# A chunked gated recurrence in front of two expert layers: inclusive gate sums, column pairs on TensorE, rows and logits in one product, and elementwise work on GpSimd

## The chip, the core and the metric

The kernel runs on one core of a Trainium2 chip. A core has five engines that run side by side and wait for one another through semaphores: TensorE (PE in the profile; PEld is its weight load), VectorE (DVE), ScalarE (ACT), GpSimd (POOL) and SyncE (SP), which here issues most of the transfers. The metric is the device time of one execution in microseconds.

## The reference

Three stages follow one another. Only the first is changed.

```python
def _attn_ref(q, k, v, f_logit):            # (4, 8, 768, 48) each
    f = 1.0 / (1.0 + np.exp(-f_logit))
    for t in range(S):
        state = f[:, :, t, :, None] * state + np.einsum('bhd,bhe->bhde', k[:, :, t], v[:, :, t])
        y[:, :, t] = np.einsum('bhd,bhde->bhe', q[:, :, t], state)

def _moe_ref(x, ...):                       # x: (3072, 384), 8 experts, 2 per token
    noisy_logits = x @ w_gate + np.log1p(np.exp(x @ w_noise)) * noise
    # the two best experts per token, softmax over the two
    # out += weight * (relu(x @ w1[e]) @ w2[e])

def _moe2_ref(x, ...):                      # rms norm, then a gated feed-forward layer, width 1536
    return (silu(xn @ w_gate) * (xn @ w_val)) @ w_out
```

## The kernel before

The recurrence is cut into 24 chunks of 128 positions: 4 batches of 6 chunks, all 8 heads at a time. The heads lie in pairs (HP = 4 pairs): one head of a pair on partitions 0 to 63 (48 of them used), the other on 64 to 127. A chunk n passes through these steps, each a function in the code:

- `decay`: the gates' logarithms and their running sum along the chunk. A clip (L325, VectorE), an exponential and a logarithm (L327, L329, ScalarE), a scan (L331, VectorE). Tile `cs`.
- `prep`: keys times exp(sum), queries times exp(-sum): `KT` (L358) and `QT` (L363), both on VectorE.
- `keys`: the keys turned by TensorE, copied to `Ks`.
- `scores`: the products of keys and queries, 8 heads (L384), in two halves; VectorE multiplies each of two banks by the causal mask, `AM` (L389).
- `state`: keys times values, for a pair of heads in one product (L398); `carry` adds the old state on VectorE (`su`, L413) and scales it on GpSimd (`Ss`, L415). In the first chunk of a batch VectorE does it alone, in the last there is none.
- `inter`: queries times old state (L424), and `attend`: masked scores times values (L432), into the same bank; four heads of one side are taken first, then four of the other. ScalarE copies the bank to `yT`.
- `rows`: the result turned and written to memory (`xd`); `logit` and `logit_turn`: the routing logits as four narrow products (L453), a copy, a turn, and a sum on VectorE (L462).

After every four chunks a `router` picks the experts for 512 tokens, in parts that `safe()` takes off a list, twice in a chunk. When the first 8 chunks are routed, their tokens are fetched back by indirect transfers that GpSimd issues (L719) and turned (`turn`), and the expert layers can begin. `expert_stream` issues these: units of an upper product (N = 256 tokens, L645) and a lower one (384 columns, also L645), each product in three parts of split precision. Weights come in half-loads, split into a high and a low part by ScalarE (L207) and by VectorE or GpSimd (L209).

TensorE runs in program order. The loop at the end of the main function sets that order: at each `yield` of `gla_stream` it adds the yield's cost to a debt, and from the moment that the first tokens are turned and the list of router steps is empty, it pays the debt at half the rate (RATIO = 0.5) with pieces of `expert_stream`. So expert products stand between the recurrence's. After the last chunk expert work runs alone. The orders of VectorE, ScalarE and GpSimd come from a scheduler, and stand fixed in the program too.

## Time and profile before

| | |
|---|---|
| median of 3 runs | 1114.31 us (1112.85 to 1114.65) |
| the profiled execution, own time | 1113.67 us |
| its span, first to last instruction | 1111.9 us |
| PE, DVE, ACT, POOL busy | 1071.9, 695.3, 490.6, 355.8 us |
| matmul records | 6861 |

The profile is one execution. Its page gives busy shares; a busy PE is not PE at its peak, since matmuls overlap. Windows give the busy time of each engine in a stretch; the timeline lists instructions in order of time; lines group instructions of one code line and one shape.

### The profile page before, as it was taken

To read this page: it belongs to the slowest core of one execution; us is meant where nothing else is said; L and a number is where in the kernel's file an instruction comes from. 1 tells how busy PE (TensorE), PEld (TensorE's weight loads), DVE (VectorE), ACT (ScalarE), POOL (GpSimd) and SP (SyncE) were. 2 spreads that over 40 slices of the span, in tenths; PEclk is the share of its full clock that TensorE was granted. 3 is DMA by queue.
4 is the path that set the end of the run, shared out by engine and by line. 5 is a ranking of instruction groups with operands and counts; after the bars stand their busy time and mean duration, and the time that the engine had idled before them with its cause. 6 is when DMAs were issued, how large, how long until landed. Compare 5 with 4: busy or idle time off the path is not lost.

```text
span 1111.9 us, 18697 instructions
## 1 busy us (share of the span) xinstructions
PE 1071.9 (96%) x6861; PEld 969.2 (87%) x6861; DVE 695.3 (63%) x1637; ACT 490.6 (44%) x1148; POOL 355.8 (32%) x415
## 2 busy tenths in 40 slices
PE   8999997999999999999999999999999999999997
PEld 5787777999989999999999988788888888888886
DVE  7999986977777554565666769745345344354332
ACT  5766543566655443444454555423223223232211
POOL 5544622434354434444546433120030020110000
PEclk9999998999999999999999999999999999999999
DMA  9986612677776443444443434120020110110001
GB/s 293 259 256 204 203 45 61 220 250 242 244 231 207 155 126 89 143 140 129 153 150 120 152 122 135 43 71 15 1 86 1 41 45 1 57 29 1 29 1 32
DMA packets 104873, 133.00 MB, mean 120 GB/s; under 512 B 8576, under 2 KB 80788, under 8 KB 104772
## 3 DMA queue, kind: packets, MB, share of 16 engines
q1 hardware_dynamic: 95203, 112.28, 31.5%
q0 software_dynamic: 9568, 19.43, 6.4%
q8 instruction: 56, 0.92, 0.3%
q14 instruction: 46, 0.37, 0.1%
HBM read 107.66 MB, written 24.02 MB: 118 GB/s over the span
## 4 chain that ended last, share of the span: by engine, by line
PE 67%; DVE 10%; DMA 10%; ACT 5%; issue 4%; POOL 3%; SPq 0%; another core or an unknown queue 0%; DVEq 0%; ACTq 0%; POOLq 0%
PE bank L645 63%; DMA raw<-in_moe_w_dram 5%; DMA xg<-xd,stoka 2%; DVE wlo L209 2%; PE bank L171 2%; PE bank L432 1%; DMA xg<-xd,stokr 1%; ACT whi L207 1%; POOL xg L719 1%; DVE AM L389 1%; DVE cs L331 1%; DVE xlo L633 1%; POOL Ss L415 1%; ACT L L327 1%; POOL hs L337 1%
## 5 line engine op out<-in xcount | busy, mean ns | idle before, releaser
L645 PE MATMUL bank<-xhi,whi 128*128 128x256 f32 (+8 forms) x1008 | 335.7, 333 | 2.2 <-ACT xhi L632 1.6
L645 PE MATMUL bank<-xlo,whi 128*128 128x256 f32 (+8 forms) x1008 | 334.9, 332 | 0.6 <-DVE xlo L633 0.5
L645 PE MATMUL bank<-xhi,wlo 128*128 128x256 f32 (+8 forms) x1008 | 334.7, 332 | 0.0
L645 PE MATMUL bank<-whi,hhi 128*128 128x384 f32 (+2 forms) x728 | 246.8, 339 | 8.1 <-ACT y L764 6.1
L645 PE MATMUL bank<-whi,hlo 128*128 128x384 f32 (+2 forms) x728 | 245.5, 337 | 0.0
L645 PE MATMUL bank<-wlo,hhi 128*128 128x384 f32 (+2 forms) x728 | 245.1, 337 | 0.0
L645 PEld LDWEIGHTS bank<-xhi,whi 128*128 128x128 f32 x1008 | 190.1, 189 | 22.4 <-ACT xhi L632 2.5
L645 PEld LDWEIGHTS bank<-xhi,wlo 128*128 128x128 f32 x1008 | 190.3, 189 | 17.3
L645 PEld LDWEIGHTS bank<-xlo,whi 128*128 128x128 f32 x1008 | 190.0, 189 | 16.9 <-DVE xlo L633 1.2
L719 POOL DMA_INDIRECT xg<-xd,stokr x139 | 133.9, 963 | 153.3 <-ACT hhi L747 125.2
L748 DVE SCALAR_TENSOR_TENSOR hlo<-bank,hhi 128x256 fp32r<-128x256 f32 (+7 forms) x192 | 83.2, 434 | 113.0 <-ACT hhi L747 92.2
L645 PEld LDWEIGHTS bank<-whi,hhi 128*128 128x128 f32 (+2 forms) x728 | 133.4, 183 | 13.8 <-ACT y L764 7.7
L209 DVE TENSOR_TENSOR wlo<-raw,whi 128x384 fp32r<-128x384 f32 (+1 forms) x312 | 135.6, 472 | 12.0 <-ACT whi L207 7.4
L747 ACT ACTIVATE hhi<-bank 128x256 fp32r<-128x256 f32 (+7 forms) x192 | 74.8, 389 | 147.3 <-PE bank L645 127.7
L645 PEld LDWEIGHTS bank<-wlo,hhi 128*128 128x128 f32 (+2 forms) x728 | 133.4, 183 | 6.2
L207 ACT ACTIVATE whi<-raw 128x256 fp32r<-128x256 f32 (+1 forms) x320 | 127.0, 452 | 24.7 <-DMA raw<-in_moe_w_dram 22.1
L645 PEld LDWEIGHTS bank<-whi,hlo 128*128 128x128 f32 (+2 forms) x728 | 132.8, 182 | 3.3
L838 DVE TENSOR_TENSOR sg<-bank,sg 128x512 f32<-128x512 f32 x72 | 49.7, 690 | 117.3 <-ACT sg L837 117.3
L789 POOL DMA_INDIRECT xg<-yd,slots x40 | 44.3, 1107 | 241.2 <-ACT hhi L841 207.6
L837 ACT ACTIVATE sg<-bank 128x512 f32<-128x512 f32 x72 | 43.0, 597 | 143.1 <-PE bank L645 134.4
L841 ACT ACTIVATE hhi<-sg 128x512 fp32r<-128x512 f32 x72 | 45.4, 630 | 116.2 <-DVE sg L839 116.0
L719 POOL DMA_INDIRECT xg<-xd,stoka x64 | 65.8, 1029 | 80.8 <-ACT hhi L747 68.4
(170 smaller groups left out, 1184.5 us busy)
## 6 DMA issues: line engine op xcount, KB each, us to landing
raw<-in_moe_w_dram SPq DMA_DIRECT2D x64, 768.0 KB
kq<-in_kq_dram SPq DMA_DIRECT2D x23, 512.0 KB
yd<-y SPq DMA_DIRECT2D x48, 192.0 KB
ft<-in_f_logit_dram SPq DMA_DIRECT2D x23, 256.0 KB
Vs<-in_v_dram SPq DMA_DIRECT2D x24, 192.0 KB
xd<-x SPq DMA_DIRECT2D x24, 192.0 KB
raw<-in_moe_w_gate_dram SPq DMA_DIRECT2D x6, 768.0 KB
raw<-in_moe_w_val_dram SPq DMA_DIRECT2D x6, 768.0 KB
```

The source lines that it names most:

```text
L171: nc.tensor.transpose(p, x, i)
L207: nc.scalar.activation(hi[:, j], raw[:, j], AF.Copy)
L209: e.tensor_tensor(lo[:, j], raw[:, j], hi[:, j].bitcast(F32), op=OP.subtract)
L327: nc.scalar.activation(l, f, AF.Exp, scale=-1.0)
L645: nc.tensor.matmul(o, a, b, start=start and i == 0, stop=stop and i == 2)
L719: paced(nc.gpsimd.indirect_dma_start(out=b.xg[i][:, k_], out_offset=None, in_=table, in_offset=bass.IndirectOffsetOnAxis(ap=rows_of[:, k_, ...
L747: mark[0] = nc.scalar.activation(hhi[:, :N], p[:, :N], AF.Relu).ins
L748: mark[1] = nc.vector.scalar_tensor_tensor(hlo[:, :N], p[:, :N], 0.0, hhi[:, :N].bitcast(F32), op0=OP.max, op1=OP.subtract).ins
L789: paced(nc.gpsimd.indirect_dma_start(out=y, out_offset=None, in_=ya if n < GROUP else yd, in_offset=bass.IndirectOffsetOnAxis(ap=at_, axis ...
L837: nc.scalar.activation(sg, ps[0], AF.Sigmoid)
L838: nc.vector.tensor_tensor(sg, ps[0], sg, op=OP.mult)
L841: mark[0] = nc.scalar.activation(hhi, sg, AF.Copy).ins
```

## The change

The running sum now takes in the gate of the chunk's first position, so that the chunk's own total is the last column of exp(-sum): GpSimd copies it to `hs` and `carry` multiplies by it, and the four small instructions that made the weight `w` go. The sum's cap becomes a cap of 4.7e18 on exp(sum), within the key product. The clip of the gates goes from VectorE to GpSimd, as do the query product of every odd chunk and one product of five of the six routings. The scores of 8 heads go to one tile of two banks and are masked by one instruction. `state` and `attend` take the two heads of a pair one after the other, each on its own half of TensorE's columns; `carry` works on the two halves of the partitions apart. `rows` and the logits come from one product of `yT` with a matrix of 96 picking and 16 weight columns (`columns`). The order in a chunk is scores, rows, inter, keys, state, attend, and routing, fetches, weight loads and turns are put one to four chunks earlier. The key product becomes a scalar-tensor-tensor instruction.

```diff
-GATE_MAX, GATES_MAX = 39.0, 60.0
+GATES_MAX = 42.0
+KEYS_MAX = 4.7e18
...
-    ROUTE = (0, 2, 4)
+    ROUTE = (0, 1, 2)
...
-    BANK = {"T": "04", "t": "0", "A0": "1", "A1": "2", "Y": "3", "U": "5", "X": "7", "R": "6"}
-    SHARED = {"T": "0", "A0": "1", "A1": "2", "Y": "3", "U": "7", "X": "7", "R": "0",
-              "h": "4", "t": "0", "acc": "56"}
+    BANK = {"T": "0", "K": "4", "t": "0", "Y": "3", "U": "5", "X": "7", "R": "6"}
+    SHARED = {"T": "0", "K": "7", "Y": "3", "U": "0", "R": "7", "h": "4", "t": "0", "acc": "56"}
...
-        nc.vector.tensor_scalar(f, f, -GATE_MAX - 1.0, None, op0=OP.max)
+        nc.gpsimd.tensor_scalar(f, f, -GATES_MAX - 1.5, None, op0=OP.max)
         yield
         nc.scalar.activation(l, f, AF.Exp, scale=-1.0)
         yield
         nc.scalar.activation(l, l, AF.Ln, bias=1.0)
         yield
         nc.vector.tensor_tensor_scan(cs.rearrange("p a t -> p (a t)"),
-                                     l.rearrange("p a t -> p (a t)"),
-                                     chain[:, s].rearrange("p a t -> p (a t)"), 0.0,
-                                     op0=OP.add, op1=OP.min)
-        yield
-        if s.stop == HP:
-            nc.gpsimd.tensor_copy(hs[:, 0, n], st["L", n][:, :, 0])
-            nc.gpsimd.tensor_copy(hs[:, 1, n], st["cs", n][:, :, P - 1])
-            if n % NCH:
-                e = wk.tile([P, HP], F32, name="e", bufs=3)
-                nc.gpsimd.tensor_tensor(e, hs[:, 1, n - 1], hs[:, 0, n], op=OP.add)
-                nc.scalar.activation(e, e, AF.Exp, scale=-1.0)
-                w = wk.tile([P, HP, 2], F32, name="w", bufs=4)
-                nc.gpsimd.tensor_tensor(w, e[:, :, None].to_broadcast([P, HP, 2]),
-                                        upper[:, None, :].to_broadcast([P, HP, 2]), op=OP.mult)
-                st["w", n - 1] = w
+                                     chain[:, s].rearrange("p a t -> p (a t)"),
+                                     l.rearrange("p a t -> p (a t)"), 0.0,
+                                     op0=OP.mult, op1=OP.add)
...
-        st["K"] = nc.vector.tensor_tensor(st["KT", n][:, s], Ek, st["kq", n][:, s, 0],
-                                          op=OP.mult).ins
+        st["K"] = nc.vector.scalar_tensor_tensor(st["KT", n][:, s], Ek, KEYS_MAX,
+                                                 st["kq", n][:, s, 0], op0=OP.min,
+                                                 op1=OP.mult).ins
         yield
         st["e"] = nc.scalar.activation(cs, cs, AF.Exp, scale=-1.0).ins
         yield
-        nc.vector.tensor_tensor(st["QT", n][:, s], cs, st["kq", n][:, s, 1], op=OP.mult)
+        (nc.gpsimd if n % 2 else nc.vector).tensor_tensor(
+            st["QT", n][:, s], cs, st["kq", n][:, s, 1], op=OP.mult)
+        if s.stop == HP:
+            nc.gpsimd.tensor_copy(hs[:, n], st["cs", n][:, :, P - 1])
...
-    def scores(n, part):
+    def scores(n):
         QT = st["QT", n]
         KT = st["KT", n]
-        if part == 0:
-            st["pA", n] = [cut(bank(f"A{g}"), HP, P) for g in range(2)]
-        ps = st["pA", n]
-        for h in range(4 * part, 4 * part + 4):
+        p = pa.tile([P, 2, HP, P], F32, name="scores")
+        for h in range(H):
             o = 64 * (h % 2)
-            nc.tensor.matmul(ps[h % 2][:, h // 2, :], KT[o:o + D, h // 2, :],
+            nc.tensor.matmul(p[:, h % 2, h // 2, :], KT[o:o + D, h // 2, :],
                              QT[o:o + D, h // 2, :], start=True, stop=True)
-        if part:
-            for g in range(2):
-                t = wk.tile([P, HP, P], F32, name=f"AM{g}")
-                nc.vector.tensor_tensor(t, ps[g], mask[:, None, :].to_broadcast([P, HP, P]),
-                                        op=OP.mult)
-                st["AM", n, g] = t
+        t = st["AM", n] = wk.tile([P, H, P], F32, name="AM")
+        nc.vector.tensor_tensor(t, p.rearrange("p g a t -> p (g a) t"),
+                                mask[:, None, :].to_broadcast([P, H, P]), op=OP.mult)
...
-        pU = cut(bank("U"), HP, 2 * D)
+        pU = cut(bank("U"), HP, D)
         for a in range(HP):
-            nc.tensor.matmul(pU[:, a], Ks[n % NK][:, 2 * a:2 * a + 2, :],
-                             Vs[n % NV][:, 2 * a * D:2 * (a + 1) * D], start=True, stop=True)
+            for g in range(2):
+                h = 2 * a + g
+                nc.tensor.matmul(pU[64 * g:64 * (g + 1), a], Ks[n % NK][:, h],
+                                 Vs[n % NV][:, h * D:(h + 1) * D], start=True, stop=True,
+                                 skip_group_check=True)
...
-        w = st["w", n]
-        sn = Ss[(c + 1) % 2].rearrange("p a b d -> p (a b) d")[:, :, :D]
-        u = st["pU", n].rearrange("p a (b d) -> p (a b) d", b=2)
-        wb = w.rearrange("p a b -> p (a b)")[:, :, None].to_broadcast([P, H, D])
-        if c:
-            t = wk.tile([P, H, D], F32, name="su", bufs=1)
-            nc.vector.tensor_tensor(t, u, Ss[c % 2].rearrange("p a b d -> p (a b) d")[:, :, :D],
-                                    op=OP.add)
-            st["C"] = nc.gpsimd.tensor_tensor(sn, t, wb, op=OP.mult).ins
-        else:
-            nc.vector.tensor_tensor(sn, u, wb, op=OP.mult)
+        u = st["pU", n]
+        t = None if c == 0 else wk.tile([P, HP, D], F32, name="su", bufs=1)
+        for g in range(2):
+            o = slice(64 * g, 64 * (g + 1))
+            wb = hs[o, n, :, None].to_broadcast([64, HP, D])
+            sn = Ss[(c + 1) % 2][o, :, g, :D]
+            if c:
+                nc.vector.tensor_tensor(t[o], u[o], Ss[c % 2][o, :, g, :D], op=OP.add)
+                st["C"] = nc.gpsimd.tensor_tensor(sn, t[o], wb, op=OP.mult).ins
+            else:
+                nc.vector.tensor_tensor(sn, u[o], wb, op=OP.mult)
...
-    def attend(n, g):
+    def attend(n):
         c = n % NCH
         pY = st["pY", n]
-        for h in range(g, H, 2):
-            nc.tensor.matmul(pY[64 * g:64 * (g + 1), h // 2, :], Vs[n % NV][:, h * D:h * D + 64],
-                             st["AM", n, g][:, h // 2, :], start=not c and h == g,
-                             stop=h == H - 2 + g, skip_group_check=True)
-        if g:
-            y = wk.tile([P, HP, P], F32, name="yT")
-            nc.scalar.activation(y, pY, AF.Copy)
-            st["yT", n] = y
+        for a in range(HP):
+            for g in range(2):
+                h = 2 * a + g
+                nc.tensor.matmul(pY[64 * g:64 * (g + 1), a, :], Vs[n % NV][:, h * D:h * D + 64],
+                                 st["AM", n][:, g * HP + a, :], start=not c and a == 0,
+                                 stop=a == HP - 1, skip_group_check=True)
+        y = wk.tile([P, HP, P], F32, name="yT")
+        nc.scalar.activation(y, pY, AF.Copy)
+        st["yT", n] = y
...
-        p = cut(bank("T"), HP, P)
+        p = cut(bank("T"), HP, NX + 2 * E)
         for a in range(HP):
-            flip(p[:, a, :], y[:, a, :], ident)
-        x = wk.tile([P, H, D], F32, name="x")
-        nc.scalar.activation(x, p.rearrange("p a (b d) -> p (a b) d", b=2)[:, :, :D], AF.Copy)
-        nc.sync.dma_start(xd[n * P:(n + 1) * P, :], x)
-
-    def logit(n):
-        y = st["yT", n]
-        p = cut(bank("X"), P)
-        for a in range(HP):
-            nc.tensor.matmul(p[32 * a:32 * (a + 1), :], wgn[:, a, :], y[:, a, :],
-                             start=True, stop=True, skip_group_check=True)
-        t = wk.tile([P, P], F32, name="lgT")
-        nc.scalar.activation(t, p, AF.Copy)
-        st["lgT", n] = t
-
-    def logit_turn(n):
-        p = cut(bank("X"), P)
-        flip(p, st["lgT", n], ident)
-        nc.vector.tensor_reduce(lg[:, n], p.rearrange("p (a e) -> p e a", a=HP)[:, :2 * E],
-                                axis=AX.X, op=OP.add)
+            nc.tensor.matmul(p[:, a, :], y[:, a, :], columns[:, a, :], start=True, stop=True)
+        x = wk.tile([P, HP, NX], F32, name="x")
+        nc.scalar.activation(x, p[:, :, :NX], AF.Copy)
+        nc.sync.dma_start(xd[n * P:(n + 1) * P, :], x.rearrange("p a x -> p (a x)"))
+        nc.vector.tensor_reduce(lg[:, n], p.rearrange("p a e -> p e a")[:, NX:], axis=AX.X,
+                                op=OP.add)
...
+        (nc.gpsimd if n1 < NT else V).tensor_tensor(
+            rh, rh, names[:, 2 * n0:2 * n1, None].to_broadcast([P, 2 * ng, nst]), op=OP.mult)
...
-                scores(i, 0)
-                safe()
-                yield 0.87
-                scores(i, 1)
-                yield 0.87
+                scores(i)
+            safe()
+            yield 1.1
             if i == 0:
                 run(prep, 1)
                 for n in range(2, GATES):
                     after_prep(decay, n)
-            if valid(i):
-                state(i)
-                yield 0.86
-            safe()
             if valid(i - 1):
                 rows(i - 1)
-                yield 0.43
+                yield 1.0
             if valid(i):
                 inter(i)
-                carry(i)
-                yield 0.87
-            if valid(i - 1):
-                logit(i - 1)
-            if valid(i):
-                attend(i, 0)
-                yield 0.8
+                yield 1.0
+            safe()
             if valid(i + AHEAD):
                 run(prep, i + AHEAD)
             if valid(i + 1):
                 keys(i + 1)
-                yield 0.43
+                yield 0.5
             if valid(i):
-                attend(i, 1)
-                yield 0.57
-            if valid(i - 1):
-                logit_turn(i - 1)
+                state(i)
+                carry(i)
+                attend(i)
+                yield 1.6
...
-            if i in (6, 8):
+            if i in (4, 6):
                 start_loads()
-            if 8 <= i < 16:
+            if 6 <= i < 14:
                 take_part(0)
...
 
     for m in range(NT // GROUP - 1):
-        i = m * GROUP + GROUP + 2
+        i = m * GROUP + GROUP + 1
         for o in ROUTE + ((ROUTE[-1] + 1,) if (m + 1) * GROUP == NTA else ()):
             at(i + o, lambda m=m: route(m))
-    for j, fns in enumerate(blocks[0].fetches):
-        for k_, fn in enumerate(fns):
-            at(16 + j, fn)
-    for fn in blocks[0].turns:
-        at(19, fn)
+    for i, fn in enumerate(blocks[0].fetches + [blocks[0].turns]):
+        at(13 + i, lambda fns=fn: [fn() for fn in fns])
```

TensorE, one chunk early in the program, before and after. Banks are matmul results; `ident` marks a turn.

```order
L398 MATMUL bank_370<-Vs_125,Ks_122 128x96 x4
L171 MATMUL bank_375<-ident,yT 128x128 x4
L424 MATMUL bank_383<-QT,Ss_130 128x128 x4
L453 MATMUL bank_391<-yT,wgn 32x128 x4
L432 MATMUL bank_383<-AM_366,Vs_125 64x128 x4
L171 MATMUL bank_409<-ident,KT 128x128 x4
L432 MATMUL bank_383<-AM_368,Vs_125 64x128 x4
L171 MATMUL bank_421<-ident,lgT 128x128
```

```order
L380 MATMUL scores<-QT,KT 128x128 x8
L442 MATMUL bank_342<-columns,yT 128x112 x4
L421 MATMUL bank_351<-QT,Ss_132 128x128 x4
L173 MATMUL bank_364<-ident,KT 128x128 x4
L394 MATMUL bank_370<-Vs_127,Ks_124 64x48 x8
L431 MATMUL bank_351<-AM,Vs_127 64x128 x8
```

Before, the eight score products (four rows to a bank, not shown) precede these; the state product stood ahead of `inter` and the two halves of `attend` apart. Now state and attend stand together at the end, with narrow products, two for each pair.

GpSimd, where the first expert units stand beside the recurrence (late chunks), before and after. L719 and L702 are the indirect loads of expert tokens, Ss the new state.

```order
L415 TENSOR_TENSOR Ss_129<-su,w 128x8x48
L719 DMA xg<-xd,stoka 128x96
L338 COPY hs<-cs 128x4
L415 TENSOR_TENSOR Ss_130<-su,w 128x8x48
L415 TENSOR_TENSOR Ss_129<-su,w 128x8x48
L415 TENSOR_TENSOR Ss_130<-su,w 128x8x48
L719 DMA xg<-xd,stoka 128x96 x56
```

```order
L412 TENSOR_TENSOR Ss_131<-su,hs 64x4x48 x2
L702 DMA xg<-xd,stoka 128x96 x4
L211 TENSOR_TENSOR wlo_1857<-raw,whi_1856 128x256
L702 DMA xg<-xd,stoka 128x96
L358 TENSOR_TENSOR QT<-cs,kq 128x512
L361 COPY hs<-cs 128x4
L412 TENSOR_TENSOR Ss_132<-su,hs 64x4x48 x2
```

The loads for expert units stood behind the last state; now they stand between states, with weight splits and query products.

## Rows read from the trace of the kernel before

**Rows 1.** windows, all engines; stretch, us, busy us (records), clock, DMA share, GB/s

```profile
7.20:120.40 113.20, 105.32 (x1011) 86.55 (x1010) 105.55 (x251) 75.36 (x178) 55.82 (x104) 0.98 0.87 256
120.40:174.10 53.70, 50.18 (x520) 42.20 (x519) 43.93 (x127) 25.40 (x62) 23.29 (x35) 1.00 0.31 93
174.10:183.10 9.00, 3.17 (x38) 2.56 (x37) 4.74 (x18) 2.91 (x9) 3.03 (x4) 0.84 0.15 44
```

**Rows 2.** windows, the score products of L384 alone

```profile
7.20:120.40 113.20, 20.22 (x257) 16.20 (x257) 0.98 0.87 256
```

**Rows 3.** timeline, PE, one chunk; start us, us, instruction

```profile
154.81 1.16 PE L384 MATMUL bank<-QT,KT 48*128 48x128 f32 x16
155.91 1.13 PE L398 MATMUL bank<-Vs,Ks 128*128 128x96 f32 x8
156.87 0.60 PE L171 MATMUL bank<-ident,yT 128*128 128x128 f32 x4
157.31 1.06 PE L424 MATMUL bank<-QT,Ss 128*128 128x128 f32 x8
158.30 0.43 PE L453 MATMUL bank<-yT,wgn 128*32 128x128 f32 x8
158.65 1.09 PE L432 MATMUL bank<-AM,Vs 128*64 128x128 f32 x8
159.67 0.66 PE L171 MATMUL bank<-ident,KT 128*128 128x128 f32 x4
160.26 1.09 PE L432 MATMUL bank<-AM,Vs 128*64 128x128 f32 x8
161.28 0.33 PE L171 MATMUL bank<-ident,lgT 128*128 128x128 f32 x1
161.53 0.71 PE L384 MATMUL bank<-QT,KT 48*128 48x128 f32 x8
```

**Rows 4.** timeline, PE, late chunks

```profile
165.54 1.58 PE L432 MATMUL bank<-AM,Vs 128*64 128x128 f32 x16
170.47 0.28 PE L645 MATMUL bank<-xhi,whi 128*128 128x256 f32 x1
170.59 0.28 PE L645 MATMUL bank<-xlo,whi 128*128 128x256 f32 x1
```

**Rows 5.** lines, DVE, 7.2 to 174.1; shapes, count, busy us, mean ns, idle before

```profile
L389 DVE TENSOR_TENSOR AM<-bank,mask 128x512 f32<-128x512 f32 x48 | 31.1, 677 | 2.2 <-PE bank L384 2.2
L363 DVE TENSOR_TENSOR QT<-cs,kq 128x512 f32<-128x512 f32 x23 | 17.0, 741 | 1.1 <-ACT cs L361 1.1
L325 DVE TENSOR_SCALAR ft<-ft 128x512 f32<-128x512 f32 x23 | 12.0, 529 | 0.0
L413 DVE TENSOR_TENSOR su<-bank,Ss 128x384 f32<-128x384 f32 x16 | 8.7, 546 | 0.0
L541 DVE TENSOR_TENSOR r_rh<-r_rh,names 128x448 f16<-128x448 f16 x4 | 3.0, 748 | 0.0
```

**Rows 6.** lines, POOL, 7.2 to 174.1

```profile
L415 POOL TENSOR_TENSOR Ss<-su,w 128x384 f32<-128x384 f32 x16 | 21.7, 1357 | 30.0 <-DVE su L413 13.4 <-DVE r_oh L521 5.6 <-DVE r_mx L482 4.7
L209 POOL TENSOR_TENSOR wlo<-raw,whi 128x384 fp32r<-128x384 f32 x4 | 4.5, 1131 | 1.5 <-ACT whi L207 1.4
L118 POOL CAST irowh<-irow 128x128 f16<-128x128 f32 x1 | 0.3, 333 | 0.0
```

**Rows 7.** timeline, DVE and POOL, three places

```profile
111.57 1.21 POOL L415 TENSOR_TENSOR Ss<-su,w 128x384 f32<-128x384 f32 x1 [1.71 <-DVE su L413]
112.01 1.05 DVE L325 TENSOR_SCALAR ft<-ft 128x512 f32<-128x512 f32 x1
...
118.17 0.41 DVE L325 TENSOR_SCALAR ft<-ft 128x512 f32<-128x512 f32 x1
...
158.32 0.83 POOL L415 TENSOR_TENSOR Ss<-su,w 128x384 f32<-128x384 f32 x1 [4.72 <-DVE r_mx L482]
```

**Rows 8.** timeline, POOL, an indirect load

```profile
173.36 0.94 POOL L719 DMA_INDIRECT xg<-xd,stoka  x1 [0.30 <-issue]
```

More of the change, by code (lines that the diff above doesn't have):

```diff
@@ L1 @@
+import math
 from contextlib import ExitStack
@@ L90, in tile_gated_attention_moe_ffn @@
     ones = cp.tile([P, P], BF16, name="ones")
-    upper = cp.tile([P, 2], F32, name="upper")
     names = ep.tile([P, 2 * NT], F16, name="names")
@@ L105, in constants @@
         yield
-        nc.vector.memset(upper, 0.0)
-        nc.vector.memset(upper[0:64, 0:1], 1.0)
-        nc.vector.memset(upper[64:128, 1:2], 1.0)
+        nc.gpsimd.tensor_copy(
+            pick_x.rearrange("p a (b d) -> p a b d", b=2),
+            ident.rearrange("p (b d) -> p b d", b=2)[:, None, :, :D].to_broadcast([P, HP, 2, D]))
         yield
@@ L155, in bank @@
             i = turns[use] = turns.get(use, -1) + 1
-        return pp.tile([P, 512], F32, name="bank" + b[i % len(b)])
+        k_ = b[i % len(b)]
+        return (late["pp"] if k_ in "12" else pp).tile([P, 512], F32, name="bank" + k_)
     def cut(t, *dims):
@@ L271, in tile_gated_attention_moe_ffn @@
     chain = gp.tile([P, HP, P], F32, name="chain")
-    wgn = gp.tile([P, HP, 32], F32, name="wgn")
+    NX = 2 * D
+    columns = gp.tile([P, HP, NX + 2 * E], F32, name="columns")
+    pick_x = columns[:, :, :NX]
+    pa = gla.enter_context(tc.tile_pool(name="pa", bufs=1, space=PSUM))
     NK, NV = AHEAD + 1, LOADS + 2
@@ L369, in keys @@
             return
-        p = cut(bank("T"), HP, P)
+        p = cut(bank("K"), HP, P)
         for a in range(HP):
@@ L440, in rows @@
     def rows(n):
         y = st["yT", n]
-        p = cut(bank("T"), HP, P)
+        p = cut(bank("T"), HP, NX + 2 * E)
         for a in range(HP):
-            flip(p[:, a, :], y[:, a, :], ident)
-        x = wk.tile([P, H, D], F32, name="x")
-        nc.scalar.activation(x, p.rearrange("p a (b d) -> p (a b) d", b=2)[:, :, :D], AF.Copy)
-        nc.sync.dma_start(xd[n * P:(n + 1) * P, :], x)
-    def logit(n):
-        y = st["yT", n]
-        p = cut(bank("X"), P)
-        for a in range(HP):
-            nc.tensor.matmul(p[32 * a:32 * (a + 1), :], wgn[:, a, :], y[:, a, :],
-                             start=True, stop=True, skip_group_check=True)
-        t = wk.tile([P, P], F32, name="lgT")
-        nc.scalar.activation(t, p, AF.Copy)
-        st["lgT", n] = t
@@ L616, in check @@
         bad = rp.tile([P, 4], F32, name="bad")
-        for c, most in enumerate((GATE_MAX, GATES_MAX)):
-            V.tensor_reduce(bad[:, c:c + 1], hs[:, c].rearrange("p n a -> p (n a)"), axis=AX.X,
-                            op=OP.max)
-            V.tensor_scalar(bad[:, c:c + 1], bad[:, c:c + 1], most, None, op0=OP.is_gt)
+        V.tensor_reduce(bad[:, 1:2], hs.rearrange("p n a -> p (n a)"), axis=AX.X, op=OP.min)
+        for c in range(2):
+            V.tensor_scalar(bad[:, c:c + 1], bad[:, 1:2], math.exp(-GATES_MAX), None, op0=OP.is_lt)
         V.tensor_reduce(bad[:, 2:3], early, axis=AX.X, op=OP.max)
@@ L1023, in gla_stream @@
             load_f(3)
-            nc.sync.dma_start(wgn, moe_w_both)
+            nc.sync.dma_start(columns[:, :, NX:], moe_w_both[:, :, :2 * E])
             for t in Vs:
@@ L1136, in tile_gated_attention_moe_ffn @@
     banks[0] = FULL
+    late["pp"] = main.enter_context(tc.tile_pool(name="pp2", bufs=1, space=PSUM))
     wp2 = main.enter_context(tc.tile_pool(name="wp2", bufs=1))
```

10 lines of the change are left out of this document (4 added, 6 removed).

## The prediction

> **What bounds the kernel now.** I read the page first. PE is busy 96% of the span, but that is a mean over two stages: a recurrence of 24 chunks up to 174 us, in which hardly any expert work runs, and expert layers afterwards, which the change doesn't touch. So time can be gained in two ways: a shorter recurrence, or expert work done inside it. I then took windows over the recurrence. Chunks 0 to 15 take 113.2 us [rows 1]: the score products have 16 records a chunk and 257 stand in that window [rows 2], so it is 16 chunks of 7.07 us. In it PE is busy 105.32 us and DVE 105.55 us [rows 1]: 6.58 and 6.60 us a chunk, both 93%. Neither has room, so a chunk gets shorter only if both get less to do. Chunks 16 to 23 take 53.7 us, 6.71 us each, and there DVE is down to 82%, since the gates and keys of later chunks are done, while PE stays at 93% [rows 1]. From 174.1 to 183.1 the last results and routing steps follow one another with PE busy 3.17 of 9.00 us [rows 1]. Expert work at its full rate starts at 183.1 us; until then two upper units are done, 18 products of 0.12 us from start to start [rows 4], 2.2 us.
>
> The timeline of one chunk without routing shows what PE does, by the starts [rows 3]: scores 1.10, state 0.96, rows 0.44, inter 0.99, logits 0.35, attend 1.02, keys 0.59, attend 1.02, turn of the logits 0.25; 6.72 us in all. I use starts and not durations, since each group's last matmul overlaps the next group.
>
> **PE, part by part.** Scores 1.10, inter 0.99 and keys 0.59 stay. The logits' 0.35 and the turn's 0.25 go. The turn of rows becomes a full product with 112 columns, shaped like inter with 128: 0.99 x 112/128 = 0.87 (bounds: 0.44, as the turn, and 0.99, as inter). Attend now alternates between the two halves of the columns. Where its halves happened to follow each other directly, 16 passes took 1.58 us, against 1.09 for 8 [rows 3, 4]; the second half cost only 0.49. The halves overlap, then, and finer alternation should let them do so throughout. I take 1.10, the time of the 16 alternating passes of the scores (bounds 1.02 and 1.58). State becomes 16 passes of half the width instead of 8: between 0.48, half of today's, and 1.92, twice; no row shows it. I take 0.65, near the lower end, as the alternating passes are the nearest row. Sum: 1.10 + 0.87 + 0.99 + 0.59 + 0.65 + 1.10 = 5.30 us, 1.4 us less than now.
>
> **DVE, part by part, per chunk.** The clip goes: 12.0 us in 23 instructions, 0.52 each [rows 5]. Half the query products go: 0.741/2 = 0.37. One routing product of 0.748 goes in five of the six routings, 0.16 per chunk. Two maskings of 0.677 become one of twice the size: between no gain and 0.2; I take 0.10. The addition of 0.546 is cut into two on half the partitions, each with half the columns: between no loss and 0.546; I take 0.10 over the chunks, since only 16 of 24 have it. The key product keeps its size and its place, and the scan also: nothing. Sum: 6.60 - 0.52 - 0.37 - 0.16 - 0.10 + 0.10 = 5.55 us.
>
> **What GpSimd gives back.** It gets the clip: 128x512 with one input. A conversion of 128x128 took 0.333, the nearest row with one input [rows 6]; by width it would be 1.33, without growth 0.33, and I take the middle, 0.8 (upper bound 1.5, a two-input product of this width). The query product: a two-input product of 128x384 took 1.131, so 1.51, every second chunk 0.75 [rows 6]. The routing product about 0.3 a chunk. Together 1.85 us more, while four tiny instructions go. GpSimd has room (55.82 of 113.2 us busy), but not beside every DVE instruction. A clip on DVE that started 0.44 us after a state product on GpSimd took 1.05 us and ended 0.28 us after that product did (113.06 and 112.78 us); another took 0.41 [rows 7]. The state product takes 0.83 left alone and 1.357 on average [rows 6, 7]. They exclude each other. Today this costs the clips 0.529 - 0.41 = 0.12 us on average for 0.55 us of state products per chunk: a fifth. A fifth of 1.85 is 0.35 (bounds: nothing, if all of it falls beside DVE's PSUM work, and 1.85). DVE: 5.9 us a chunk, more than PE's 5.3, so DVE sets the pace in chunks 0 to 15. At the present 93% that is 6.3 us.
>
> **The sum.** Chunks 0 to 15: 16 x 6.3 = 101 us, from 7.2 to 108 us. By the order of the changed program, 108 upper products (256 columns, 0.12 us) and 54 lower ones (384 columns, 0.18 by width) then stand between the recurrence's matmuls before its last attend: 13.0 + 9.7 = 22.7 us. Chunks 16 to 23: 8 x 5.30 = 42.4, less 2.5 for two chunks without state and keys, plus 22.7 = 62.6 us of PE work; at 93%, 67.4 us. The recurrence ends at 175.6 us. The tail with its PE idle time is gone, as the last routing steps of the loop are due in chunks 21 to 23 instead of 22 to 26, and expert work fills the rest. Against now: 183.1 - 175.6 = 7.5 us earlier, and 22.7 - 2.2 = 20.5 us of expert work ahead. 28 us in all. 1111.9 - 28 = 1083.9 us of span; the execution's own time lies 1.8 us above its span and 0.6 below the median, so 1086 us.
>
> Transfers: DMA is 87% busy in chunks 0 to 15 [rows 1] at 256 GB/s. A chunk needs 1.15 MB, 4.5 us at that rate, below 6.3; weights that start earlier add some. I cost it at nothing; if chunks fell to 5.5 us, DMA would be next.
>
> **Rivals.** *The lock (20%).* GpSimd's new work doesn't fit beside DVE's PSUM instructions; most of the 1.85 us comes back as waiting, on either engine. Rows 7 speak for it, and that GpSimd was idle half the time against it. DVE at 6.5 us and 93%: 7.0 us a chunk, 112 us; the late chunks at 9.0, 72 us, since weight splits on GpSimd come in there: end at 191 us, 8 later than 183.1, with 20.5 us ahead: 12.5 us gained, 1101 us. The Trainium skill, page "SBUF — State Buffer", section "Who interferes with whom", states that GpSimd shares a pair of SBUF ports with DVE as an exclusive lock, held for the whole instruction, against any DVE instruction with two SBUF inputs. By that rule moving the clip off DVE would free nothing where scan and key product follow each other closely; this trace agrees as to the blocking [rows 7], not as to how often it strikes. By the rule in full the time is this rival's, by the fifth of above the forecast's.
>
> *PE sets the pace (20%).* The lock costs nothing, and the early chunks run at 5.3/0.93 = 5.7: 91 us; the late ones at 96%, 65 us: end at 163.5, 40 us gained, 1074 us.
>
> *The column halves don't overlap (4%).* Attend stays at 2.04 and state takes 1.3: PE 6.9 us, 7.07 a chunk as now, the late chunks 78 us or more: end at 198 us, 5 us gained, 1109 us. The 1.58 us of rows 4 speaks against it.
>
> *Slower: the state's round trip (6%).* State product, addition on DVE, scaling on GpSimd and inter follow each other, and now only attend, scores and rows, some 3 us of PE, lie between state and the next inter; before, it was nearly a whole chunk. The scaling queues behind clips, query products and, in late chunks, up to five indirect loads of 0.94 + 0.30 us [rows 8]. In early chunks: 0.65 + 0.65 + 1.5 behind a query product + 2.7 for two scalings both blocked like today's 1.357 + 0.99 + 0.59 keys = 7.1 us; with 6.2 us of loads in front, over 10 in late ones. It decides if the round trip exceeds 6.3 us in most chunks, and makes the kernel slower when early chunks average 7.6 and late ones 10: end at 209 us, 26 later, 20.5 ahead: 1119 us. Against it: only 16 of 24 chunks have the trip, and expert products lengthen the slack in late chunks.
>
> **Numbers.** The forecast itself has 50%, 1078 to 1094 us. With the lock and PE as bound the range is 1070 to 1106 us; outside are the unpaired halves, the slow round trip and the ends of the two rivals. 0.2% (about what a measurement tells from no change) is 2 us. Faster 0.92, the same 0.03, slower 0.05.
>
> **What would show it.** Attend near 1.1 us in the timeline, state near 0.65, a rows product near 0.9: PE's part. Chunks 0 to 15 in 101 us with DVE above 90% busy: DVE's part; if DVE is below 85% there and PE waits for Ss, it is the round trip; if clips or scans are stretched beside GpSimd, the lock. Upper products between scores from chunk 15 on, PE above 90% there, and no idle stretch after the last attend. The forecast is wrong if the recurrence ends after 190 us, or if a later stage gives the lead back, by waiting for weights before 300 us.

## The result, and the profile after

The changed kernel takes 1130.9 us (median of 4 runs, 1127.8 to 1132.1) against 1114.5 before: a ratio of 1.014 (95% interval 1.012 to 1.016). The forecast was 1086 us, range 1070 to 1106. Its profiled execution has a span of 1129.5 us, 17.6 more than before.

The two stages of the recurrence, in the windows of the changed kernel (columns as in [rows 1]), end where the scores of chunk 16 begin and behind the last rows product:

```profile
8.20:149.30 141.10, 91.65 (x1071) 82.36 (x1070) 110.52 (x239) 80.26 (x163) 97.95 (x112) 0.82 0.73 215
149.30:217.50 68.20, 66.00 (x702) 60.74 (x701) 50.94 (x142) 31.62 (x78) 39.21 (x47) 0.97 0.41 128
```

The first row holds 258 records of the scores, as many as [rows 2] plus one: chunks 0 to 15 take 141.1 us, forecast 101, before 113.2 [rows 1]. Chunks 16 to 23, with expert work between their products, take 68.2 us; forecast 67.4. (To their last attend, where the forecast stops counting, it is 65.2 us, with 169 expert products before it, forecast 162.) So the first 16 chunks alone take 40 us more than forecast, where the whole kernel takes 45 more. There PE is busy 65%, DVE 78% and POOL 69%: nothing is full, so the engines wait for one another. TensorE is granted 0.82 of its clock: over a third of the stretch is at the lower level of 1.2 GHz.

A chunk in which PE waits for only one thing (timeline of PE in the changed kernel; before in [rows 3]):

```profile
119.25 1.16 PE L380 MATMUL scores<-QT,KT 48*128 48x128 f32 x16
120.34 1.15 PE L442 MATMUL bank<-columns,yT 128*128 128x112 f32 x8
121.32 1.07 PE L421 MATMUL bank<-QT,Ss 128*128 128x128 f32 x8
122.23 0.60 PE L173 MATMUL bank<-ident,KT 128*128 128x128 f32 x4
122.76 0.67 PE L394 MATMUL bank<-Vs,Ks 128*64 128x48 f32 x16
124.61 1.09 PE L431 MATMUL bank<-AM,Vs 128*64 128x128 f32 x16 [1.18 <-DVE AM L383]
125.64 1.16 PE L380 MATMUL scores<-QT,KT 48*128 48x128 f32 x16
```

By the starts: scores 1.09, rows 0.98, inter 0.91, keys 0.53, state 0.67 without the wait, attend 1.03: 5.21 us, forecast 5.30, before 6.72. PE got as short as expected. What it waits for up to 150 us (what waits, for what; us in total, times, longest):

```profile
PE bank L533 <- POOL r_rh L527: 22.8, 3, 10.6
PE bank L173 <- DVE KT L352: 13.4, 2, 12.0
PE bank L442 <- ACT yT L435: 10.2, 5, 3.3
PE bank L431 <- DVE AM L383: 2.8, 2, 1.6
```

Two of these have one plain cause each. *The start.* GpSimd (its timeline) holds the clip of chunk 1 as the third; the two ahead of it are those of chunks 2 and 3, whose gates were requested last and landed at 11.27 us:

```profile
11.34 2.94 POOL L331 TENSOR_SCALAR ft<-ft 128x512 f32<-128x512 f32 x2 [6.53 <-DMA ft<-in_f_logit_dram]
14.23 0.19 POOL L361 COPY hs<-cs 128x4 f32<-128x4 f32 x1
14.37 0.49 POOL L107 COPY columns<-ident 128x384 f32<-128x384 f32 x1
14.84 1.48 POOL L331 TENSOR_SCALAR ft<-ft 128x512 f32<-128x512 f32 x1
```

Chunk 1's scan then starts at 17.67 us and PE, done at 9.4, turns keys at 21.37. *The routing product.* PE, then GpSimd, around the longest wait:

```profile
64.28 1.16 PE L380 MATMUL scores<-QT,KT 48*128 48x128 f32 x16
76.09 0.53 PE L533 MATMUL bank<-r_rh,r_ol 128*128 128x56 f16 x8 [10.65 <-POOL r_rh L527]
76.44 2.03 PE L442 MATMUL bank<-columns,yT 128*128 128x112 f32 x8
```

```profile
71.81 1.57 POOL L211 TENSOR_TENSOR wlo<-raw,whi 128x256 fp32r<-128x256 f32 x1 [2.57 <-ACT whi L209]
73.35 1.79 POOL L331 TENSOR_SCALAR ft<-ft 128x512 f32<-128x512 f32 x1
75.11 0.93 POOL L527 TENSOR_TENSOR r_rh<-r_rh,names 128x448 f16<-128x448 f16 x1
```

The product waits behind a weight split, which waits for ScalarE, and a clip; rows, inter and all else of PE stand behind it. The rows product takes 2.03 us there instead of 1.15: half the clock, after ten idle microseconds. The clip lasts 1.48 us at best (forecast 0.8); on DVE it was 0.41 undisturbed [rows 7].

### The profile page after: what moved, and what is told of

Read it like the earlier page. It is cut to its first block, busy times and chain, and to the rows that moved or that the text cites. A ratio compares the mean times of both kernels' runs of the same rounds, so it can differ in the third digit from the quotient of the medians.

```text
span 1129.5 us, 18724 instructions
## 1 busy us (share of the span) xinstructions
PE 1052.9 (93%) x6901; PEld 960.8 (85%) x6901; DVE 683.7 (61%) x1576; ACT 485.7 (43%) x1104; POOL 402.6 (36%) x421
## 4 chain that ended last, share of the span: by engine, by line
PE 70%; DVE 9%; DMA 8%; issue 4%; POOL 4%; ACT 3%; SPq 1%; DVEq 0%; POOLq 0%; ACTq 0%
PE bank L628 64%; DMA raw<-in_moe_w_dram 4%; DMA xg<-xd,stoka 2%; POOL xg L702 2%; DVE wlo L211 2%; PE bank L442 2%; PE bank L173 1%; PE bank L421 1%; DMA xg<-xd,stokr 1%; DVE cs L337 1%; PE bank L431 1%; POOL ft L331 1%; DVE cv L180 1%; DMA ft<-in_f_logit_dram 1%; ACT whi L209 1%
## 5 line engine op out<-in xcount | busy, mean ns | idle before, releaser
L702 POOL DMA_INDIRECT xg<-xd,stokr x139 | 134.9, 970 | 154.2 <-ACT hhi L730 124.4
L211 DVE TENSOR_TENSOR wlo<-raw,whi 128x256 fp32r<-128x256 f32 (+1 forms) x301 | 135.6, 487 | 15.9 <-ACT whi L209 10.1
L824 ACT ACTIVATE hhi<-sg 128x512 fp32r<-128x512 f32 x72 | 45.4, 631 | 116.5 <-DVE sg L822 116.3
L702 POOL DMA_INDIRECT xg<-xd,stoka x64 | 67.1, 1048 | 65.0 <-ACT hhi L730 42.2
```

The lines of the kernel that those rows point to most:

```text
L211: e.tensor_tensor(lo[:, j], raw[:, j], hi[:, j].bitcast(F32), op=OP.subtract)
L702: paced(nc.gpsimd.indirect_dma_start(out=b.xg[i][:, k_], out_offset=None, in_=table, in_offset=bass.IndirectOffsetOnAxis(ap=rows_of[:, k_, ...
L824: mark[0] = nc.scalar.activation(hhi, sg, AF.Copy).ins
```

## The experiments

Ratios are to the kernel before on the same chip, with the 95% interval; 0.001 is 1.1 us. "All on DVE" means clips, queries and the routing product on VectorE.

**The engines and the plan.** Four edits of the changed kernel.

e_clip, all clips back on VectorE:

```diff
-        nc.gpsimd.tensor_scalar(f, f, -GATES_MAX - 1.5, None, op0=OP.max)
+        nc.vector.tensor_scalar(f, f, -GATES_MAX - 1.5, None, op0=OP.max)
```

> The changed kernel with all 24 clips back on VectorE; nothing else differs. Theory (GpSimd's in-order queue): the clip takes 1.48 us there and stands in front of other work; chunk 1's scan moves from 17.67 back to about 10 us, ScalarE's 13.8 us of waits for clipped gates go, and the routing product has less in front of it. About 15 to 25 us less than the changed kernel: 1106 to 1116. Rival (the lock between GpSimd and VectorE alone): VectorE gets 23 x 0.41 = 9.4 us more, GpSimd 34 us less; stretched scans become 1.2 us again, and the time falls by some 5 us: 1122 to 1128. Rival (the earlier routing and loads): no change, 1128 to 1134.

Measured: 1.000 (0.998 to 1.002), 1114.3 us. As the theory said; the rival, sharing alone, is out.

e_rh, the routing product back:

```diff
-        (nc.gpsimd if n1 < NT else V).tensor_tensor(
+        V.tensor_tensor(
             rh, rh, names[:, 2 * n0:2 * n1, None].to_broadcast([P, 2 * ng, nst]), op=OP.mult)
```

> The changed kernel with the routing product (five of six groups) back on VectorE, nothing else. Theory (GpSimd's queue): the three waits of PE for it, 22.8 us in all, go, and with them some stretches at half clock behind them; VectorE takes 5 x 0.75 us more. 10 to 20 us less: 1111 to 1121. Rival (the earlier plan: routing steps one chunk apart instead of two, weights two chunks earlier, make PE wait whichever engine does the product): PE waits at the same place for another tile, 1126 to 1133.

Measured: 1.011 (1.008 to 1.013). The rival is right: PE waits as long, now for VectorE:

```profile
PE bank L533 <- DVE r_rh L527: 21.0, 3, 7.8
PE bank L173 <- DVE KT L352: 13.7, 2, 12.1
```

e_dve, both of these and:

```diff
-        (nc.gpsimd if n % 2 else nc.vector).tensor_tensor(
+        nc.vector.tensor_tensor(
             st["QT", n][:, s], cs, st["kq", n][:, s, 1], op=OP.mult)
```

> The changed kernel with all three moves to GpSimd undone: clips, odd query products and routing products on VectorE; the PE part, the inclusive sums and the earlier plan stay. Theory (GpSimd's queue is what lost the time): VectorE is back at some 6.6 us a chunk, so chunks 0 to 15 take about what they took before, 113 to 118 us instead of 141, and the expert work inside the recurrence stays ahead: 1092 to 1106, faster than the kernel before. Rival (the PE part or the plan lose it, by round trip or clock): 1120 to 1135.

Measured: 0.997 (0.996 to 0.999), 1110.6 us: a little faster than before, but less than expected. Chunks 0 to 15 take 126.1 us, not 113 to 118; the waits at the routing product stay, 19.9 us up to 150 us.

e_plan, the plan of before:

```diff
-    ROUTE = (0, 1, 2)
+    ROUTE = (0, 2, 4)
-        i = m * GROUP + GROUP + 1
+        i = m * GROUP + GROUP + 2
-            if i in (4, 6):
+            if i in (6, 8):
-            if 6 <= i < 14:
+            if 8 <= i < 16:
...
```

and the first block's fetches from chunk 16 on, its turn at 19, as before.

> The changed kernel with the plan of before: routing steps two chunks apart and one chunk later, weights requested at chunks 6 and 8 instead of 4 and 6, their splits and the first block's fetches later by two to three chunks. Theory (GpSimd's queue): the routing product has more time to come through, so part of the 22.8 us of PE's waits for it goes, the start and the clips stay as they are, and less expert work is ready inside the recurrence: 1115 to 1130. Rival (the earlier plan is what lost it): PE's waits for the routing product go, and so do the stalls, 1095 to 1105.

Measured: 1.013 (1.010 to 1.016), no gain. The routing waits shrink to 8.9 us (up to 220 us, since the steps come later), but the 12.3 us at the start stay, and the first expert product moves from 146 to 181 us. Neither theory holds alone: there are several losses.

**One loss at a time.** e_start repairs the start, e_space the distance of the routing steps:

```diff
-        nc.gpsimd.tensor_scalar(f, f, -GATES_MAX - 1.5, None, op0=OP.max)
+        (nc.vector if n < 4 else nc.gpsimd).tensor_scalar(f, f, -GATES_MAX - 1.5, None, op0=OP.max)
```

```diff
-    ROUTE = (0, 1, 2)
+    ROUTE = (0, 1, 3)
-        at(13 + i, lambda fns=fn: [fn() for fn in fns])
+        at(14 + i, lambda fns=fn: [fn() for fn in fns])
```

> The changed kernel with the clips of chunks 0 to 3 on VectorE, the other 20 on GpSimd as changed. In the changed kernel GpSimd's order has the clips of chunks 2 and 3, whose transfers land at 11.3 us, ahead of the clip of chunk 1, whose gates were there by 7.8 us. Theory: this start alone costs 7 to 9 us: chunk 1's scores at 16 to 18 us instead of 25.2, and the time 1121 to 1125. Rival (later waits take it up, since PE waits at the routing steps anyway): 1128 to 1131.

> The changed kernel with the third routing step one chunk later and nothing else. Theory: the 22.8 us of PE's waits for the routing product go to 5 or less and the time falls to 1112 to 1120; what is left over the kernel before is the start (8 us) and the clips in GpSimd's queue. Rival (GpSimd's queue, and not the distance of the steps, makes the product late): the waits stay above 10 us, 1124 to 1131.

Measured: 1.004 (1.003 to 1.005) and 1.004 (1.002 to 1.006). Each alone is worth 11 us. e_startspace has both edits:

> The changed kernel with both repairs: clips of chunks 0 to 3 on VectorE and the third routing step a chunk later; the other clips, the odd queries and the routing products stay on GpSimd. Each repair alone gave a ratio of 1.004 to the kernel before, from 1.014. Theory (two separate losses): they add up, 1.014 - 0.010 - 0.010 = 0.994, 1107 to 1111, the same as with everything on VectorE, so GpSimd's share in itself gives and costs nothing. Rival (GpSimd's moves do take VectorE's load off once the two losses are gone, as forecast): 1085 to 1100. Rival (they overlap): 1114 to 1119.

Measured: 1.005 (1.003 to 1.007). They don't add up; where one wait goes, another takes its place. GpSimd and PE in e_startspace:

```profile
25.22 3.72 POOL L331 TENSOR_SCALAR ft<-ft 128x512 f32<-128x512 f32 x2 [3.24 <-DMA ft<-in_f_logit_dram]
28.91 1.26 POOL L358 TENSOR_TENSOR QT<-cs,kq 128x512 f32<-128x512 f32 x1
30.12 0.65 POOL L361 COPY hs<-cs 128x4 f32<-128x4 f32 x1
30.74 2.00 POOL L412 TENSOR_TENSOR Ss<-su,hs 64x192 f32<-64x192 f32 x2
```

```profile
32.79 1.44 PE L421 MATMUL bank<-QT,Ss 128*128 128x128 f32 x5 [5.45 <-POOL Ss L412]
```

Two clips wait for gates, a query follows, and the scaled state that PE needs comes last. e_dvespace takes the close steps apart with all on DVE:

> The changed kernel with clips, odd queries and routing products on VectorE, and the third routing step one chunk later (steps in chunks 0, 1, 3 of a group instead of 0, 1, 2; the first block's fetches one chunk later too). Theory now: the routing chain of VectorE between the second and the third step takes some 10 us beside its chunk work, PE arrives after 5 us and waits. With a chunk more the 21.1 us of waits for the routing product go, with the stretches at half clock behind them: 15 to 20 us less than with the same engines and the close steps (1110.6), 1091 to 1096, and chunk 16 starts at about 113 us instead of 133. Rival (VectorE's amount of work sets the pace, and the waits only show where it falls due): the waits move to the maskings and yT, 1106 to 1111.

Measured: 0.994 (0.992 to 0.996), 1110.3 us. The waits for the routing product go, those for the maskings grow to 13.6 us: as the rival said. Chunks 0 to 15 in its windows, and in those of e_noclip, with the line of the clip deleted:

```profile
7.30:123.80 116.50, 87.83 (x1054) 76.91 (x1053) 108.51 (x258) 71.26 (x146) 40.25 (x72) 0.90 0.86 254
```

> The same kernel (all on VectorE, third routing step a chunk later) with the clip of the gates left out altogether: 24 instructions of 0.41 to 0.50 us less on VectorE, nothing more on GpSimd. It bounds what a move of the clip can give. Theory (VectorE sets the pace): 16 chunks by 0.46 = 7 us less up to chunk 16 and some 2 after: 1101 to 1105. Rival (the chain through PE and ScalarE sets it): within 2 us of 1110.

```profile
6.90:120.50 113.60, 89.97 (x1052) 79.27 (x1051) 100.71 (x240) 71.89 (x150) 41.93 (x74) 0.88 0.90 263
```

Measured: 0.992 (0.989 to 0.994). With everything on DVE it is 93% busy, 7.3 us a chunk, and PE only 75%. Without the clip DVE has 7.8 us less to do; the stretch gets 2.9 us shorter and the kernel 2.6 (uncertain by 3.6). Neither theory fits whole. Up to chunk 12 DVE does set the pace: chunk 8 starts at 58.6 us instead of 63.5, chunk 12 at 88.4 instead of 93.6. Then part of this is lost in one wait of PE:

```profile
115.06 2.08 PE L421 MATMUL bank<-QT,Ss 128*128 128x128 f32 x8 [5.99 <-POOL Ss L412]
```

In front of that scaling GpSimd has four indirect loads, which the earlier plan puts between the states. In e_dvespace the same wait is 3.4 us. So in this plan a move of the clip gives little, even if it were free.

**What the clip costs on GpSimd.** In the kernel before, e_bclip moves the clips of chunks 4 to 23, e_b8 those of 8 to 23 (`n < 8`); e_8space is e_startspace with `n < 8`:

```diff
-        nc.vector.tensor_scalar(f, f, -GATE_MAX - 1.0, None, op0=OP.max)
+        (nc.vector if n < 4 else nc.gpsimd).tensor_scalar(f, f, -GATE_MAX - 1.0, None, op0=OP.max)
```

> The kernel before with one edit: the clips of chunks 4 to 23 on GpSimd. The move by itself, without the PE part and without another plan. Forecast's model: VectorE loses 0.52 us a chunk and gets a fifth of GpSimd's time back as waiting (0.3 of 1.5 us), but PE at 6.6 us a chunk stays: 1110 to 1114. Theory (the clip takes 1.6 us there and stretches VectorE's scan and products by about as much as it took off): no gain, 1114 to 1122.

> The kernel before with the clips of chunks 8 to 23 on GpSimd, those of the first eight on VectorE (with the first four alone on VectorE the ratio was 1.013). Theory (an instruction that waits for its transfer on GpSimd blocks what stands behind it, and in the first chunks, where the DMA engines are full, the gates come late): from chunk 8 on the gates are there in time, the loss of 14 us goes, ratio 0.997 to 1.004. Rival (the clip costs in every chunk, 1.6 us in GpSimd's order and stretched VectorE work beside it): two thirds of the loss stay, 1.007 to 1.012.

> The changed kernel with the third routing step a chunk later and the clips of chunks 0 to 7 on VectorE, 8 to 23 on GpSimd (with chunks 0 to 3 alone on VectorE the ratio was 1.005, and PE waited 10.0 us for the scaled state that stood behind clips). Theory (blocked queue in the first chunks): GpSimd's waits for gates and PE's for the state go, ratio 0.992 to 0.998, at least as good as with everything on VectorE (0.994). Rival (the clip costs in every chunk): 1.001 to 1.006.

Measured: 1.013 (1.010 to 1.016), 1.007 (1.004 to 1.009) and 1.001 (1.000 to 1.002). So half of the loss in the kernel before hangs on the four clips of chunks 4 to 7, half on the 16 others; neither theory takes all. How the first of them does it shows in e_bclip, on GpSimd, VectorE and PE:

```profile
15.74 1.50 POOL L325 TENSOR_SCALAR ft<-ft 128x512 f32<-128x512 f32 x1 [4.96 <-DMA ft<-in_f_logit_dram]
```

```profile
20.17 0.47 DVE L115 TENSOR_SCALAR sel<-sel,pcol 128x512 f16<-128x512 f16 x1 [7.39 <-POOL sel L114]
```

```profile
21.47 2.08 PE L384 MATMUL bank<-QT,KT 48*128 48x128 f32 x16 [5.77 <-DVE QT L363]
```

A clip of a later chunk waits 4.96 us for its gates. Behind it on GpSimd stands a table (`sel`), for which VectorE waits; behind that on VectorE stands the query product of chunk 1, for which PE waits. Chunk 2 then starts 6.9 us later than before (30.63 against 23.75 us).

e_dummy leaves all on DVE, steps apart, and adds on GpSimd:

```diff
+        if n >= 4:
+            nc.gpsimd.tensor_scalar(spare, f, -GATES_MAX - 1.5, None, op0=OP.max)
```

> All elementwise work on VectorE, the third routing step a chunk later (ratio 0.994), and for chunks 4 to 23 a second clip of the same gates on GpSimd into a tile that nobody reads, after VectorE's own clip. It never waits for a transfer and nothing waits for its result; it only occupies GpSimd for 1.5 us and shares the memory with VectorE. Theory (the clip loses because GpSimd, and what stands behind in its order, waits for gates): ratio 0.993 to 0.997. Rival (the time that the clip takes on GpSimd and from VectorE beside it is the loss, whoever needs the result): 1.000 to 1.006, with VectorE's scans and products stretched and chunk 16 after 127 us.

Measured: 1.004 (1.003 to 1.005), against 0.994 without. By the ratios, twenty instructions whose result nobody needs cost 11 us. Chunks 0 to 15 in e_dummy, and PE's waits for the state up to 140 us, in e_dvespace and in e_dummy:

```profile
7.20:128.00 120.80, 91.19 (x1052) 80.00 (x1051) 111.46 (x259) 71.03 (x146) 62.84 (x86) 0.86 0.83 243
```

```profile
PE bank L421 <- POOL Ss L412: 4.3, 2, 3.4
```

```profile
PE bank L424 <- POOL Ss L415: 9.5, 5, 3.9
```

The stretch is 4.3 us longer (120.8 against 116.5). VectorE is busy 3.0 us longer with one instruction more: it is stretched beside GpSimd. PE's waits for the state grow by 5.2 us, but only two of them, 1.3 us together, have a clip right in front of the scaling. Two long ones, 3.3 and 3.9 us, stand behind indirect loads, as in e_dvespace and e_noclip. The longest, on GpSimd:

```profile
133.79 0.51 POOL L415 TENSOR_TENSOR Ss<-su,hs 64x192 f32<-64x192 f32 x1 [3.70 <-DMA xg<-xd,stoka]
```

Where the other 7 of the 11 us go isn't shown.

**Transfers, clock, work on PE.** e_dvez is e_dvespace with the zero fill of 1.5 MB later:

```diff
-            if i == 3:
+            if i == 14:
                 nc.sync.dma_start(yd.rearrange("(e s) d -> s e d", e=E)[min(CAPS):],
```

> All elementwise work on VectorE, the third routing step a chunk later (ratio 0.994), and the zero fill of 1.5 MB issued in chunk 14 instead of chunk 3. In the first 53 us the DMA engines are as good as full (share 1.01 at 298 GB/s). Rival (transfers set the pace of the first eight chunks): 1.5 MB less there are 5 us, chunk 8 at 58 to 60 us instead of 63.5, ratio 0.989 to 0.991. Theory (VectorE, 94% busy there, sets it): chunk 8 within 2 us of 63.5, ratio 0.992 to 0.996.

Measured: 0.993 (0.990 to 0.995), chunk 8 at 63.8 us: as the theory said, 1.5 MB less give nothing there. e_fill is the changed kernel with a busy PE in the first wait:

```diff
+            if i == 0:
+                warm(46)
             if valid(i + 1):
                 keys(i + 1)
```

> The changed kernel with 46 bf16 products of 128x512 whose result nobody reads, in PE's queue ahead of the key turn of chunk 1, where PE waits 12.0 us (9.4 to 21.4 us) in the changed kernel: about 10 us of work at the full clock. The wait itself stays. Theory (an idle PE is granted the lower clock, and that costs time of its own): the 13.7 us at half clock that begin at 11.8 us go, chunk 3 starts 3 to 6 us earlier than at 37.3 us, ratio 1.007 to 1.012 instead of 1.014. Rival (the clock costs nothing, since VectorE and GpSimd set the pace): clock up, ratio 1.013 to 1.016.

```profile
9.24 10.10 PE L988 MATMUL bank<-ones 128*128 128x512 bf16 x46
34.47 2.05 PE L442 MATMUL bank<-columns,yT 128*128 128x112 f32 x8 [7.81 <-ACT yT L435]
```

Measured: 1.016 (1.014 to 1.018). Between 7 and 30 us the granted clock is 0.90 instead of 0.70, and the time doesn't move, as the rival said. But the run doesn't decide it. With the edit the scheduler also gave ScalarE another order: the copy of chunk 0's result (`yT`), at 25.74 us in the changed kernel, comes at 33.83, behind the gates of later chunks. PE waits 7.8 us for it, and chunk 2 starts at 40.5 us instead of 30.3. What the lower clock costs stays open. e_warm adds three such products ahead of rows and three ahead of attend to e_dvespace:

```diff
+                if banks[0] is BANK:
+                    warm(3)
                 rows(i - 1)
```

> All elementwise work on VectorE and the third routing step a chunk later, as in the run before (1110.3 us, ratio 0.994 to the kernel before), with six further bf16 products of 128x512 a chunk on PE whose result nobody reads, three ahead of the rows and three ahead of attend, in chunks 1 to 15: about as much PE work as the change took away (6 x 0.21 us = 1.3 us at 2.4 GHz). Theory (VectorE sets the pace in chunks 0 to 15, and what PE does in its gaps only decides its clock): the granted clock between 7 and 120 us rises from 0.90 to 0.97 or more and the time stays or falls by up to 5 us: 1105 to 1111. Rival (PE's amount of work sets the pace): 20 us of added work come back as 10 to 20 us: 1120 to 1130.

Measured: 1.002 (1.000 to 1.003), 9 us more than without, with the clock up from 0.91 to 0.94 only: added PE work does come back, by less than half. So DVE, at 93%, isn't the only limit; PE's own work counts too. e_dveplan, all on DVE with the plan of before, is the PE part and the sums alone:

> All elementwise work on VectorE and the whole plan of before (routing steps two chunks apart, weights and fetches later): the PE part and the inclusive sums alone. Theory: no routing waits and no stretched scans, chunks at VectorE's 6.6 to 7.0 us, so chunk 16 starts at 113 to 119 us (120.4 before), but hardly any expert work stands inside the recurrence; the start is 8 us earlier than in the run with the plan of before and GpSimd's clips (1131): 1112 to 1121. Rival (the earlier weights cost something by themselves, by transfers or splits between chunks): 1095 to 1108.

Measured: 1.000 (0.999 to 1.002). 1.4 us less on PE in each chunk give nothing by themselves: chunk 16 starts at 116.4 us instead of 120.4, but the recurrence's last attend ends at 174.7, as before (174.1). The last, e_best, is e_dvez with

```diff
-    for rest in (5, 6, 4, 2):
+    for rest in (3, 3, 2, 1):
```

> All elementwise work on VectorE, the third routing step a chunk later, the zero fill in chunk 14 (together 0.993), and the last group's routing steps closer behind the recurrence (3, 3, 2 and 1 units between them instead of 5, 6, 4 and 2), so that the remaining gathers stand earlier against the expert units. Theory (the lead of 13 us at the 200th expert product is given back in part because gathers and last routing come later against the expert units than before): about 3 us more of the lead stays, ratio 0.988 to 0.992. Rival (the stream of weights takes the lead back, whatever the routing does): 0.992 to 0.995.

Measured: 0.998 (0.996 to 0.999), worse than e_dvez: neither theory has that. The best kernel found that keeps the clip is e_dvez, 1102.5 us (0.993), level with e_dvespace.

## Why the prediction was wrong

- *PE, 5.30 us a chunk:* right, 5.21. *Expert work between late chunks, 67.4 us:* right, 68.2. *The halves of the columns:* they overlap, attend takes 1.03 us. *Recurrence's end, 175.6 us:* 214.5 to the last attend, 217.5 with the last rows, past the 190 at which the text called itself wrong.
- *"Chunks 0 to 15: 16 x 6.3 = 101 us"* is the step that failed; it took 141.1. It supposed that DVE runs at 93% of a smaller load, and so that work moved to GpSimd is gone. The same stretch takes 134.5 us in e_start, 129.7 in e_space, 126.8 in e_startspace, 126.1 in e_dve and 116.5 in e_dvespace. Three things stand in the forecast's place. First, the order of GpSimd's work was never looked at: the start costs 11 us of the kernel's time by e_start. Second, the closer routing steps were counted as a gain only; that VectorE needs ten microseconds for its routing chain (51.8 to 62.0 us in e_dve) and PE arrives after five costs 11 us by e_space, whichever engine does the last product (e_rh). Both repairs together give only 10 us, not 23 (e_startspace). Third, *what GpSimd gives back*: the clip was sized 0.8 and takes 1.48, and the "fifth" priced only how VectorE is stretched beside GpSimd. That was not too low (3.0 us on VectorE for 15 extra clips of 1.6 us in e_dummy, an eighth). GpSimd's queue was left out: clips that wait for gates hold what stands behind them, in e_bclip a table that VectorE needs, in e_startspace the state's scaling. With all on DVE and the steps apart the time falls by another 12 to 13 us (1.005 to 0.994).
- What is then left to the forecast is the relief of DVE itself, 7.3 instead of 6.3 us a chunk. Without the moves to GpSimd the forecast's own sum gives 6.6 us of DVE work, 7.1 us at 93%; e_dvespace has 6.8 and 7.3. e_noclip shows that even a free clip brings only 0.2 us a chunk.
- *The rivals.* The lock (1101) is there, at about the price of the forecast. On it the Trainium skill, page "SBUF — State Buffer", section "Who interferes with whom", states that a VectorE instruction with two SBUF inputs contends with a GpSimd instruction that reads SBUF. The trace agrees only in part. In the changed kernel a clip that starts at 36.78 us, inside a scan of VectorE (until 37.90 us), takes 2.40 us instead of 1.48. But here are a clip and a key product inside it, each at its normal length, on GpSimd and on VectorE:

```profile
41.30 1.49 POOL L331 TENSOR_SCALAR ft<-ft 128x512 f32<-128x512 f32 x1
```

```profile
41.95 0.68 DVE L352 SCALAR_TENSOR_TENSOR KT<-Ek,kq 128x512 f32<-128x512 f32 x1
```

  The clip that [rows 7] shows stretched on VectorE has one input, so that row bears on the blocking, not on this sentence. The state's round trip (1119) named the queue, but PE's waits for the state are 0.8 us in all in the changed kernel; they grow to 10.0 us where others are gone (e_startspace). PE as bound is out: PE is busy 65% in the first 16 chunks. What the half clock adds behind the waits isn't shown, since e_fill doesn't decide it.
- *"A later stage gives the lead back":* there is no lead to give back, and the expert layers lose more. Expert products in windows from 0 to 212 and 800 us (PE busy, count, clock, DMA) in the changed kernel, then in the kernel before:

```profile
0.00:212.00 212.00, 28.71 (x166) 0.87 0.63 187
0.00:800.00 800.00, 596.93 (x3677) 0.96 0.50 155
```

```profile
0.00:212.00 212.00, 30.65 (x201) 0.98 0.65 193
0.00:800.00 800.00, 603.40 (x3758) 0.99 0.50 155
```

  35 products behind at 212 us, 81 at 800. In time: the 200th expert product starts 8.2 us later than before, where the forecast had it 28 us earlier, the 600th 13.5 and the last one ends 17.9 us later. So 36 of the 45 us are lost by the end of the recurrence and 10 in the expert layers, which the forecast left unchanged. Most variants lose so there, e_dvespace a whole lead of 8.8 us at the 200th product; the cause stays open. A later last routing step (275 us, 232 before) doesn't explain it: in e_dveplan it comes at 233, and that kernel loses too.

## What to carry over

Moving work to a less busy engine is priced by what stands behind it in that engine's order, not by the engine's idle share: read its queue for the instruction that feeds the critical engine, and for waits on transfers in front of it. A step placed closer to its input needs the input's chain, at the pace at which a 93% busy engine runs it, as its least distance. When two engines are both full, shortening one alone can give nothing (e_dveplan). And an edit that moves one instruction can change the scheduled order of others: look for new waits before the time is put down to the edit (e_fill).

## What was not expected of the hardware

On GpSimd a one-input clip of 128x512 takes longer (1.48 us) than a two-input product of that size (1.26); on VectorE it is the other way round, 0.41 and 0.68. And a clip on GpSimd and a two-input product on VectorE can run one inside the other without either getting longer (41.30 and 41.95 us above), while another clip took 2.40 us beside a scan (36.78 us).
